# Splitting the value matmuls of a batch's last gate/value chunk into two column halves, each multiplied by its gate at once

## The chip, the cores and the metric

The kernel runs on one core of a Trainium2 chip. The metric is the time of one execution on the device in microseconds (us). Most executions of one kernel agree within about 0.3%, so medians of several runs are quoted. Kernels are compared only within the same rounds. A ratio is the mean time of one kernel's fast runs over that of the kernel before in the same rounds; it is therefore not quite the ratio of the medians quoted beside it.

The engines are named as in the profile: PE is TensorE's matmul, PEld its weight load, DVE is VectorE, ACT is ScalarE and POOL is GpSimd.

## The reference

Attention over eight batches (8 heads, 576 tokens, 16 beacon keys in front of the causal part), then a gated feed-forward block on the 4608 resulting rows:

```python
def _moe_ref(x, w_gate, w_val, w_out) -> np.ndarray:
    g = x @ w_gate
    inv_sqrt2 = np.float32(1.0 / np.sqrt(2.0))
    gelu = 0.5 * g * (1.0 + erf(g * inv_sqrt2))
    val = x @ w_val
    return (gelu * val @ w_out).astype(np.float32)
```

`x` is 4608 x 512, the gate and value weights are 512 x 1536. The kernel cuts the 1536 inner columns into 12 chunks of 128 (`fi` = 0 to 11) and the rows into groups of 512 (`CH`). There are nine such groups for eight batches.

## The kernel before

For one chunk of one group, four matmuls (`K_CHUNKS`) make the gate and four the value, each 128 x 512 in PSUM. ACT takes the GELU of the gate, and DVE multiplies value and gate into `hT_sb`, which the output matmuls (`o_ps`) read later.

```python
psum_s = ctx.enter_context(tc.tile_pool(name="psum_s", bufs=3, space=bass.MemoryType.PSUM))   # [P, 2, 512] f32 each: two banks
psum_t = ... bufs=1                                                            # one bank
psum_o = ... bufs=1                                                            # one bank
...
def part(ci, fi, w, ps, kks=range(K_CHUNKS), last=True):
    n0 = ci * CH
    for kk in kks:
        mm(ps, (wg_sb, wv_sb)[w][:, kk, fi * P : (fi + 1) * P],
           xT_sb[:, kk, n0 : n0 + CH], kk == 0, last and kk == kks[-1], ...)
...
def gated(ci, fi, v_ps, ge_sb):
    ...
    keep(nc.vector.tensor_tensor(out=h_of[ci][:, fi, :], in0=v_ps, in1=ge_sb, op=ALU.mult))
...
def gates_first(ci, *fis):
    ge_of = {}
    for fi, (pool, tag) in zip(fis, ((psum_t, "t"), (psum_o, "o"))):
        g_ps = pool.tile([P, CH], FP32, name="g_ps", tag=tag)
        part(ci, fi, 0, g_ps)
        ge_of[fi] = gelu(g_ps)
    for fi in fis:
        v_ps = psum_s.tile([P, 2, CH], FP32, name="v_ps", tag="s")[:, 0, :]
        part(ci, fi, 1, v_ps)
        gated(ci, fi, v_ps, ge_of[fi])
```

`gates_first` runs for chunks 10 and 11 of batches 1 to 6, so in six places. Right after it, PE goes on to the output matmuls of the same group and the attention scores (`s_ps`) of the next batch. The first three score groups take the three `psum_s` buffers in rotation; the third takes the one that chunk 11's value leaves.

The softmax here doesn't subtract the row's maximum and nothing guards it: scores larger than these inputs give would overflow.

## Time and profile before

| | before |
|---|---|
| median | 365.4 us (364.5 to 365.8, 3 runs at first) |
| profiled span | 363.6 us |
| PE busy | 353.7 us, 97% of the span |
| DVE, ACT, POOL busy | 45%, 53%, 44% |
| period from one place to the next | 38.78 to 38.95 us |

A busy share is an average over stages and does not say what sets the pace in one of them. A matmul's start is recorded and its end is modelled, so stalls of PE are measured below from start to start: when the next matmul would have started at the steady rate, and when it did.

### The profile page before, as it was taken

To read this page: it belongs to the slowest core of one execution; us is meant where nothing else is said; L and a number is where in the kernel's file an instruction comes from. 1 tells how busy PE (TensorE), PEld (TensorE's weight loads), DVE (VectorE), ACT (ScalarE), POOL (GpSimd) and SP (SyncE) were. 2 spreads that over 40 slices of the span, in tenths; PEclk is the share of its full clock that TensorE was granted. 3 is DMA by queue.
4 is the path that set the end of the run, shared out by engine and by line. 5 is a ranking of instruction groups with operands and counts; after the bars stand their busy time and mean duration, and the time that the engine had idled before them with its cause. 6 is when DMAs were issued, how large, how long until landed. Compare 5 with 4: busy or idle time off the path is not lost.

```text
span 363.6 us, 7732 instructions
## 1 busy us (share of the span) xinstructions
PE 353.7 (97%) x3164; PEld 187.5 (52%) x3206; DVE 163.4 (45%) x320; ACT 193.0 (53%) x252; POOL 161.3 (44%) x288
## 2 busy tenths in 40 slices
PE   7899999999999999999999999999999999999996
PEld 7664546444654455445644564446544554444443
DVE  3548746344453345434534354335443453333322
ACT  3975788237923694358633891379335953321210
POOL 8934387556536552945374545565330530000000
PEclk9999999999999999999999999999999999999999
DMA  8999999899289975999299927993795142000112
GB/s 112 174 203 204 196 121 97 125 156 199 30 128 135 215 58 71 168 217 62 56 138 205 138 38 122 162 198 35 111 147 127 15 65 113 0 2 29 58 38 108
DMA packets 160419, 41.57 MB, mean 114 GB/s; under 512 B 146944, under 2 KB 155904, under 8 KB 160384
## 3 DMA queue, kind: packets, MB, share of 16 engines
q0 software_dynamic: 104848, 19.11, 68.4%
q1 hardware_dynamic: 55536, 21.96, 30.9%
q8 instruction: 25, 0.41, 0.5%
q14 instruction: 10, 0.08, 0.1%
HBM read 38.27 MB, written 9.44 MB: 131 GB/s over the span
## 4 chain that ended last, share of the span: by engine, by line
PE 88%; DMA 5%; DVE 3%; POOL 2%; issue 1%; ACT 0%; SPq 0%; POOLq 0%
PE gv_ps L168 40%; PE o_ps L168 25%; PE x_ps L168 9%; PE s_ps L168 6%; DMA q_sb<-in_q_dram 3%; PE v_ps L168 3%; PE g_ps L168 3%; PE t_ps L176 2%; DMA k_sb<-in_k_dram 1%; DVE qkT L235 1%; POOL v_sb L111 1%; PE w_ps L168 1%; DVE o_sb L481 1%; DMA xT_sb<-y_sb 1%; POOL k_sb L111 0%
## 5 line engine op out<-in xcount | busy, mean ns | idle before, releaser
L171 ACT ACTIVATE ge_sb<-gv_ps 128x512 bf16<-128x512 f32 x95 | 55.8, 597 | 134.7 <-PE gv_ps L168 132.4
L433 DVE TENSOR_TENSOR hT_sb<-gv_ps,ge_sb 128x512 bf16<-128x512 f32 x95 | 64.9, 691 | 105.4 <-ACT ge_sb L171 105.3
L171 ACT ACTIVATE expT<-s_ps 128x992 bf16<-128x992 f32 (+3 forms) x112 | 100.5, 975 | 11.3 <-PE s_ps L168 9.8
L168 PE MATMUL gv_ps<-xT_sb,wg_sb 128*128 128x512 bf16 x378 | 105.1, 379 | 0.5
L168 PE MATMUL o_ps<-wo_sb,hT_sb 128*128 128x512 bf16 (+3 forms) x492 | 101.0, 373 | 2.3 <-DVE o_sb L481 0.9
L168 PE MATMUL gv_ps<-xT_sb,wv_sb 128*128 128x512 bf16 x364 | 101.7, 379 | 0.4
L320 POOL TENSOR_SCALAR_AFFINE_SELECT expT<-expT 128x256 bf16<-128x256 bf16 (+1 forms) x140 | 52.4, 391 | 48.4 <-ACT expT L171 47.1
L168 PEld LDWEIGHTS <-wv_sb 128*128 128x128 bf16 x432 | 42.2, 98 | 50.6
L168 PEld LDWEIGHTS <-wg_sb 128*128 128x128 bf16 x432 | 42.1, 98 | 49.9
L168 PEld LDWEIGHTS <-hT_sb 128*128 128x128 bf16 (+1 forms) x516 | 40.8, 96 | 43.8 <-issue 5.4
L168 PEld LDWEIGHTS <-expT 128*128 128x128 bf16 (+1 forms) x960 | 33.7, 97 | 9.0 <-POOL expT L320 3.1
L168 PE MATMUL x_ps<-v_sb,expT 128*128 128x65 bf16 (+1 forms) x960 | 36.8, 193 | 0.0
L111 POOL DMA_DIRECT2D v_sb<-in_v_dram x40 | 33.7, 861 | 6.1 <-DMA wv_sb<-in_moe_w_val_dram 2.4
L168 PE MATMUL s_ps<-qkT 64*128 64x80 bf16 (+5 forms) x528 | 33.1, 250 | 2.4 <-DVE qkT L239 1.6
L111 POOL DMA_DIRECT2D k_sb<-in_k_dram x30 | 25.2, 843 | 16.8 <-DMA v_sb<-in_v_dram 8.3
L111 POOL DMA_DIRECT2D q_sb<-in_q_dram x30 | 25.3, 874 | 9.9 <-DMA wo_sb<-in_moe_w_out_dram 3.6
L356 DVE TENSOR_TENSOR y_sb<-x_ps,r_sb 128x320 bf16<-128x320 f32 (+1 forms) x47 | 28.8, 612 | 1.8 <-DVE r_sb L354 0.2
L354 DVE RECIPROCAL r_sb<-x_ps 128x5 f32<-128x5 f32 (+1 forms) x47 | 9.6, 204 | 38.9 <-PE x_ps L168 38.9
L479 DVE COPY o_sb<-o_ps 128x512 f32<-128x512 f32 (+2 forms) x31 | 20.7, 668 | 13.3 <-PE o_ps L168 12.7
L168 PEld LDWEIGHTS <-qkT 64*128 64x128 bf16 x528 | 18.6, 95 | 14.0 <-issue 6.1
L399 POOL COPY hold_sb<-xT_sb 128x2 bf16<-128x2 bf16 x6 | 1.1, 186 | 31.9 <-DMA xT_sb<-y_sb 31.9
L433 DVE TENSOR_TENSOR hT_sb<-v_ps,ge_sb 128x512 bf16<-128x512 f32 x13 | 9.0, 692 | 9.5 <-PE v_ps L168 9.5
(58 smaller groups left out, 153.7 us busy)
## 6 DMA issues: line engine op xcount, KB each, us to landing
out_dram<-o_sb SPq DMA_DIRECT2D x35, 256.0 KB, 7.0
v_sb<-in_v_dram POOLq DMA_DIRECT2D x24, 128.0 KB, 9.2
q_sb<-in_q_dram POOLq DMA_DIRECT2D x18, 128.0 KB, 12.8
k_sb<-in_k_dram POOLq DMA_DIRECT2D x18, 128.0 KB, 5.5
wo_sb<-in_moe_w_out_dram POOLq DMA_DIRECT2D x3, 512.0 KB, 14.6
wg_sb<-in_moe_w_gate_dram POOLq DMA_DIRECT2D x2, 512.0 KB, 11.3
wv_sb<-in_moe_w_val_dram POOLq DMA_DIRECT2D x2, 512.0 KB, 13.1
v_sb<-in_v_dram POOLq DMA_DIRECT2D x8, 112.0 KB, 5.7
```

The lines of the kernel that those rows point to most:

```text
L111: keep(nc.gpsimd.dma_start(out=out_ap, in_=in_ap))
L168: keep(nc.tensor.matmul(out_ap, lhsT, rhs, start=start, stop=stop, **kw))
L171: keep(nc.scalar.activation(out_ap, in_ap, func, **kw))
L176: keep(nc.tensor.transpose(out_ap, in_ap, ident[0:n, 0:n]))
L235: keep(nc.vector.tensor_copy(out_ap, in_ap))
L320: nc.gpsimd.affine_select(out=d, in_=d, pattern=[[0, 2], [1, n]], compare_op=ALU.is_ge, fill=0.0, base=0, channel_multiplier=-1,)
L354: keep(nc.vector.reciprocal(r, x[:, :, :, D:DV]))
L356: nc.vector.tensor_tensor(out=y_of[i][:, :, h0:h1, :].rearrange("p j b d -> p b j d"), in0=x[:, :, :, 0:D], in1=r.to_broadcast([P, h1 - h0 ...
L399: keep(nc.gpsimd.tensor_copy(hold_sb, x[:, 0 : S : S - 1]))
L433: keep(nc.vector.tensor_tensor(out=h_of[ci][:, fi, :], in0=v_ps, in1=ge_sb, op=ALU.mult))
L479: keep(nc.vector.tensor_copy(o_ap, o_ps))
L481: keep(nc.vector.tensor_copy(o_ap, o_half))
```

## The change

Its intent: DVE should begin on chunk 11 as soon as half of it is there, so that the last product ends earlier and its PSUM buffer comes free earlier for the next batch's scores.

```diff
-    def part(ci, fi, w, ps, kks=range(K_CHUNKS), last=True):
+    def part(ci, fi, w, ps, kks=range(K_CHUNKS), last=True, c0=0, c1=CH):
...
-                xT_sb[:, kk, n0 : n0 + CH],
+                xT_sb[:, kk, n0 + c0 : n0 + c1],
...
-        keep(nc.vector.tensor_tensor(out=h_of[ci][:, fi, :], in0=v_ps, in1=ge_sb, op=ALU.mult))
+        keep(nc.vector.tensor_tensor(out=h_of[ci][:, fi, c0:c1], in0=v_ps, in1=ge_sb, op=ALU.mult))
...
-            part(ci, fi, 1, v_ps)
-            gated(ci, fi, v_ps, ge_of[fi])
+            for c0, c1 in ((0, CH),) if fi == fis[0] else ((0, CH // 2), (CH // 2, CH)):
+                part(ci, fi, 1, v_ps[:, c0:c1], c0=c0, c1=c1)
+                gated(ci, fi, v_ps[:, c0:c1], ge_of[fi][:, c0:c1], c0, c1)
```

More of the change, by code (lines that the diff above doesn't have):

```diff
@@ L428, in gelu, with gated @@
         return ge_sb
-    def gated(ci, fi, v_ps, ge_sb):
+    def gated(ci, fi, v_ps, ge_sb, c0=0, c1=CH):
         if ci not in h_of:
             h_of[ci] = hpool.tile([P, F_TILES, CH], BF16, name="hT_sb", tag="hT_sb")
-        keep(nc.vector.tensor_tensor(out=h_of[ci][:, fi, :], in0=v_ps, in1=ge_sb, op=ALU.mult))
+        keep(nc.vector.tensor_tensor(out=h_of[ci][:, fi, c0:c1], in0=v_ps, in1=ge_sb, op=ALU.mult))
     def gv_mms(ci, fi, *kks, last=False):
```

## The prediction

> **What bounds the kernel now.** I read the page first, then the chain of work by line, then the same chain in order of time, then five equal stretches of it, and last the timeline around one place that the change edits.
>
> ```profile
> PE 353.7 (97%) x3164; PEld 187.5 (52%) x3206; DVE 163.4 (45%) x320; ACT 193.0 (53%) x252; POOL 161.3 (44%) x288
> ...
> PE 88%; DMA 5%; DVE 3%; POOL 2%; issue 1%; ACT 0%; SPq 0%; POOLq 0%
> ```
>
> TensorE (PE) is busy for 97% of the span and makes up 88% of the chain that ended last. A busy PE is not yet a saturated one, so I also looked at whether anything else sets the pace from batch to batch. The next lines are the windows view, cut where the first gate matmul (g_ps) of the edited chunk pair starts in batches 1 to 6; columns are the stretch, its length, then each engine's busy time.
>
> ```profile
> 82.57:121.36 38.79, 38.36 (x345) 20.17 (x348) 17.13 (x33) 22.23 (x28) 22.25 (x39) 1.00 1.24 131
> 121.36:160.14 38.78, 38.35 (x344) 20.12 (x348) 17.14 (x33) 22.23 (x28) 21.34 (x38) 1.00 1.21 134
> 160.14:198.92 38.78, 38.35 (x344) 20.16 (x348) 17.14 (x33) 22.23 (x28) 20.89 (x38) 1.00 1.18 114
> 198.92:237.70 38.78, 38.35 (x344) 20.11 (x348) 17.13 (x33) 22.23 (x28) 20.79 (x38) 1.00 1.23 128
> 237.70:276.65 38.95, 38.52 (x344) 19.98 (x348) 17.29 (x33) 22.18 (x28) 15.85 (x32) 1.00 1.23 132
> ```
>
> Four periods agree to 0.01 us while POOL's work, which issues the loads, differs by over 1 us between them. A steady period with changing load work says that the loop through PE, ACT and DVE sets the time and no load does. That matters because the chain as printed runs through loads of q and k from 142 to 168 us; I take that part as an artefact of following POOL's queue back, since PE has no gap there.
>
> Now the edited place. The chain in order of time, for batch 2 (start, length, work):
>
> ```profile
> 121.36 1.73 PE g_ps L168 x8
> 123.09 1.73 PE v_ps L168 x8
> 124.81 0.54 PE o_ps L168 x4
> 125.35 0.71 PE s_ps L168 x14
> ```
>
> Both gate groups, both value groups (chunks 10 and 11), then the output matmuls of the same batch and the scores of the next follow without a gap: 8 matmuls in 1.73 us is 216 ns each. The timeline of the same place:
>
> ```profile
> 122.92 1.89 PE L168 MATMUL v_ps<-xT_sb,wv_sb 128*128 128x512 bf16 x8
> ...
> 124.06 0.69 DVE L433 TENSOR_TENSOR hT_sb<-v_ps,ge_sb 128x512 bf16<-128x512 f32 x1 [1.34 <-PE v_ps L168]
> 124.75 0.61 PE L168 MATMUL o_ps<-wo_sb,hT_sb 64*128 64x512 bf16 x4
> 124.92 0.69 DVE L433 TENSOR_TENSOR hT_sb<-v_ps,ge_sb 128x512 bf16<-128x512 f32 x1 [0.17 <-PE v_ps L168]
> ...
> 125.67 5.44 ACT L171 ACTIVATE expT<-s_ps 128x1024 bf16<-128x1024 f32 x6 [0.65 <-PE s_ps L168]
> ```
>
> The reader is to see three things. The two products on DVE start 0.1 us after their last matmul ends and nearly touch (124.75 against 124.92). PE does not wait for either: the output matmuls start at 124.75, before the second product has even begun. And ACT waits 0.65 us for PE's scores, so whatever delays PE here delays the softmax too.
>
> **What the Trainium skill says.** "PSUM — Partial Sum Buffer", section "PSUM bank collisions raise a hardware error", says that two engines must not touch one bank on the same 32 partitions at once, disjoint columns included, and to guard by bank, not by address. The value tile of chunk 11 is 512 fp32 columns; the page's section "Specifications (TRN2)" gives a bank as exactly 512 fp32 values, so both halves lie in one bank. The trace of before cannot show this case, because there no bank is read while more matmuls for it are to come. "VectorE: DVE Perf Modes", section "The TRN2 errata", gives (N+151)/0.96 ns for a one-element-per-cycle two-input operation. The trace agrees: 692 ns for 512 columns of the product (formula 691), and for the other product out of PSUM, 492 ns at 320 and 824 ns at 640 columns (formula 491 and 824). "TensorE: Matmul & The Clock Gate", section "Back-to-back issue gap", gives N/2.4 + 2.5 ns for a matmul at full clock, 216 ns at 512, as the chain above shows, and so 109 ns at 256; the granted clock is 1.00 in all five windows.
>
> ```profile
> L356 DVE TENSOR_TENSOR y_sb<-x_ps,r_sb 128x320 bf16<-128x320 f32 x30 | 14.8, 492 | 1.2 <-DVE r_sb L354 0.2
> L356 DVE TENSOR_TENSOR y_sb<-x_ps,r_sb 128x640 bf16<-128x640 f32 x17 | 14.0, 824 | 0.6
> ```
>
> **The change part by part.** It acts where gates_first is called: batches 1 to 6, chunk 11 only, so six places.
>
> Removed: per place 4 value matmuls of 512 columns and one product of 512 columns. Added: 8 matmuls of 256 columns, 4 more weight loads, two products of 256 columns. On PE that is 8 x 109 = 872 ns against 4 x 216 = 864 ns, about +0.01 us. The weight loads lie under the matmuls: the kernel already runs 30 x_ps matmuls of 65 columns, each with its own 128-column load, in 1.02 us, 34 ns apiece. On DVE, 2 x 425 = 850 ns against 692.
>
> Moved: the first half's product is in front of the second half's matmuls in program order. The built program, listed with its waits, has a new wait at the first matmul of the second half; counting the increments of that semaphore, it is released by the first half's product. So the read and the next write of the one bank are in sequence:
>
> ```
> Matmult v_ps<-xT_sb,wv_sb 128x256 [waits DVE]
> ```
>
> Its cost, in batch 2's times. The chunk 11 matmuls start at 123.79 (122.92 + 4 x 0.216). Four of 256 columns are issued until 124.22; the last starts at 124.11 and ends about 0.28 us later, which is the mean of the 256-column score matmuls, at 124.39. DVE is then still busy with chunk 10's product until 124.75. The first half's product starts at about 124.79 (0.04 us from one DVE operation to the next, as between the reciprocal and y_sb) and ends 0.425 us later at 125.21. From the end of a DVE operation to the matmul that waited for it takes 0.06 us, from the one such wait that recurs in this trace (o_sb ends at 128.94, the matmul starts at 129.00):
>
> ```profile
> 128.25 0.69 DVE L481 COPY o_sb<-o_ps 128x512 f32<-128x512 f32 x1 [2.64 <-PE o_ps L168]
> ...
> 129.00 1.45 PE L168 MATMUL o_ps<-wo_sb,hT_sb 128*128 128x512 bf16 x5 [0.16 <-DVE o_sb L481]
> ```
>
> So the second half starts at 125.27 in place of 124.22: PE idles for 1.05 us. All of it is on the path: before, PE went straight on to the output matmuls. With 0.01 us for the extra matmuls a place costs 1.06 us.
>
> What could be won in return is an earlier end of the last product, for whoever waits for its PSUM buffer: the third score group of the next batch (three buffers in rotation). Before, the product ended at 125.61, and that score group could start at about 125.63. There is thus at most some 0.05 us to win. After, the second half's matmuls end at about 125.88, its product runs from about 125.98 to 126.40, and the shifted score group comes at about 126.7. It is not waited for, but it was hardly waited for before. I take the gain as 0 to 0.05 us, 0.02 in the sum.
>
> Sum: 6 x (1.05 + 0.01 - 0.02) = 6.2 us. 365.4 + 6.2 = **371.6 us**, 1.7% longer.
>
> **The rivals.** First, that the intent holds: two halves let DVE start 0.43 us sooner and the next batch's scores get their buffer sooner. Against it: DVE is not free to start sooner (chunk 10's product holds it until 124.75), and nobody on PE waits for chunk 11's product. Even with no wait between the halves the gain would be at most 6 x 0.05 = 0.3 us: 365.1 us. Second, that the stall is partly hidden: behind PE's later waits for ACT, or behind loads. For it: ACT runs six exponentials without a gap after this place. Against it: ACT itself starts from PE's scores, idle 0.65 us before, so it shifts along; and the periods do not depend on the loads. If half were hidden the time would be 368.5 us. Third, that the stall is larger than worked out: a slower restart of PE after draining, or a slower hand-over between engines for this pair. 0.2 us more in each place gives 372.8 us, just beyond 2%. What speaks against it is the 0.06 us hand-over, seen with the same two engines.
>
> **Range and chances.** The wait is certain (it stands in the built program) and its length comes from durations that repeat to a few ns, so the spread is that of hidden parts and of the runs (1.3 us between lowest and highest). A range from 369.6 (a third hidden) to 373.0 (0.23 us more per place) should hold it 8 times in 10. The 2% line lies at 372.7. Faster by over 2%: 0.01. Within 2%: 0.86. Slower by over 2%: 0.13.
>
> **What would show it right or wrong.** Right: in the waits of PE a new row, v_ps waiting for DVE hT_sb, six times and about 1.0 us each, some 6 us in all; products of 256 columns at about 425 ns, 12 of them; the period between places 39.8 us; ACT idle before the first exponentials about 1.7 us in place of 0.65. Wrong: if the row is there but the period is still 38.8, the stall was hidden (second rival). If the row is missing, or far below 6 us, the wait was met early and my reading of DVE's order is wrong. If the period is over 40.0 with the row near 6 us, there is a cost after the stall that I did not see.

## The result

The changed kernel takes 370.28 us (median of 4 runs, 369.9 to 370.5) against 365.51 us, a ratio of 1.0134 with a 95% interval of 1.0117 to 1.0150. It is slower by 4.8 us, which is 0.80 us in each of the six places, and by the 2% measure it counts as the same. The time lies in the predicted range, 1.3 us below the predicted value.

The waits of PE, in the changed kernel, have a new row at the top (columns: who waited for whom, us in total, times, the longest):

```profile
PE v_ps L168 <- DVE hT_sb L433: 4.7, 6, 1.0
```

Six waits, all of the value matmuls for a product. The timeline of the same place in batch 2 of the changed kernel:

```profile
123.20 1.46 PE L168 MATMUL v_ps<-xT_sb,wv_sb 128*128 128x512 bf16 x8
...
124.33 1.02 DVE L433 TENSOR_TENSOR hT_sb<-v_ps,ge_sb 128x512 bf16<-128x512 f32 x2 [1.34 <-PE v_ps L168]
125.41 0.60 PE L168 MATMUL v_ps<-xT_sb,wv_sb 128*128 128x256 bf16 x4 [0.75 <-DVE hT_sb L433]
...
125.94 0.61 PE L168 MATMUL o_ps<-wo_sb,hT_sb 64*128 64x512 bf16 x4
126.05 0.43 DVE L433 TENSOR_TENSOR hT_sb<-v_ps,ge_sb 128x256 bf16<-128x256 f32 x1 [0.69 <-PE v_ps L168]
126.38 0.80 PE L168 MATMUL s_ps<-qkT 64*128 64x512 bf16 x14
...
126.86 1.02 ACT L171 ACTIVATE expT<-s_ps 128x1024 bf16<-128x1024 f32 x1 [1.56 <-PE s_ps L168]
```

The reader is to see that the eight value matmuls of before have become a run of eight (chunk 10 and the first half of chunk 11), a hole, and a run of four. The hole ends 0.06 us after the first half's product (124.33 + 1.02 = 125.35, then 125.41). ACT's idle time before the first exponential has grown from 0.65 to 1.56 us, so the softmax has shifted along with PE. From start to start, the first half begins at 124.06 (123.20 + 4 x 0.216) and is issued by 124.50 (4 x 0.109 later); the second half starts at 125.41. That is a stall of 0.91 us. The profile's own figure for this wait, 0.75, counts only from the modelled end of the last matmul.

The chain in order of time of the changed kernel shows which product ended it:

```profile
123.36 0.88 PE v_ps L168 x4
...
124.33 0.39 DVE hT_sb L433
124.73 0.22 issue
124.94 0.43 DVE hT_sb L433
125.37 0.04 issue
125.41 0.60 PE v_ps L168 x4
126.01 0.54 PE o_ps L168 x4
126.55 0.63 PE s_ps L168 x14
```

DVE has entered a chain that was PE alone before. Chunk 10's product runs to 125.02, and the first half's product stands behind it, from 124.94. The last line is the one gain: the block of 14 score matmuls takes 0.63 us, against 0.71 in the same view of before. In the timelines, from the block's start to the next output matmul, it is 0.63 (126.38 to 127.01) against 0.69 us (125.19 to 125.88).

The periods, in the windows view of the changed kernel cut at the same matmul as before:

```profile
82.01:121.64 39.63, 38.80 (x353) 20.29 (x352) 17.21 (x34) 22.24 (x28) 23.10 (x40) 1.00 1.22 132
121.64:161.27 39.63, 38.80 (x353) 20.28 (x352) 17.21 (x34) 22.24 (x28) 21.38 (x38) 1.00 1.21 122
161.27:201.11 39.84, 38.79 (x353) 20.28 (x352) 17.30 (x34) 22.24 (x28) 20.98 (x38) 1.00 1.18 118
```

The first two periods are 0.84 and 0.85 us longer than before, the fourth and fifth, not printed, too (39.63 and 39.79 us), and the granted clock is still 1.00. This agrees with the parts: 0.91 (stall) + 0.01 (eight smaller matmuls) - 0.06 (score block) = 0.86. The third is longer by another 0.21 us. There the two products on DVE took 1.24 us together in place of 1.02, because the second began 0.21 us later. In that stretch POOL issued three loads of k for 2.48 us without a break, but this alone does not delay DVE: at the first place of the run with two tiles (below), POOL issued four loads for 3.49 us without a break across the products, and they took their usual 1.35 us; at its third place they took 1.56. The run with two banks has the same 0.21 us at its third place and nowhere else. The cause stays open.

Six times 0.84 and the 0.21 are 5.3 us. The two profiled spans differ by 4.5, because in this run of the changed kernel the first place happened to come 0.56 us earlier (82.01 against 82.57), and the stretch from the last place to the end grew by 0.62 us only. The stretch before the first place holds no changed instruction; over all profiled runs it took from 82.0 to 83.6 us.

### The profile page after: what moved, and what is told of

Read it like the earlier page. It is cut to its first block, busy times and chain, and to the rows that moved or that the text cites. A ratio compares the mean times of both kernels' runs of the same rounds, so it can differ in the third digit from the quotient of the medians.

```text
span 368.1 us, 7822 instructions
## 1 busy us (share of the span) xinstructions
PE 355.7 (97%) x3230; PEld 187.7 (51%) x3230; DVE 163.6 (44%) x326; ACT 193.2 (52%) x252; POOL 161.5 (44%) x288
## 4 chain that ended last, share of the span: by engine, by line
PE 82%; DMA 8%; POOL 5%; DVE 3%; issue 2%; DVEq 0%; POOLq 0%
PE gv_ps L168 39%; PE o_ps L168 25%; PE x_ps L168 7%; PE s_ps L168 5%; DMA wo_sb<-in_moe_w_out_dram 4%; DMA qk<-in_q_dram 4%; PE g_ps L168 3%; PE v_ps L168 2%; POOL qk L111 1%; DVE hT_sb L433 1%; DVE o_sb L482 1%; POOL v_sb L111 1%; POOL q_sb L111 1%; POOL wg_sb L111 1%; POOL wv_sb L111 1%
## 5 line engine op out<-in xcount | busy, mean ns | idle before, releaser
L168 PE MATMUL gv_ps<-xT_sb,wv_sb 128*128 128x512 bf16 x380 | 105.3, 379 | 0.0
L168 PE MATMUL o_ps<-wo_sb,hT_sb 128*128 128x512 bf16 (+3 forms) x516 | 104.7, 373 | 0.5
L168 PEld LDWEIGHTS <-wv_sb 128*128 128x128 bf16 x456 | 44.6, 98 | 55.3 <-issue 5.7
L168 PEld LDWEIGHTS <-hT_sb 128*128 128x128 bf16 (+1 forms) x516 | 39.9, 96 | 43.1 <-issue 4.3
L168 PEld LDWEIGHTS <-qkT 64*128 64x128 bf16 x528 | 17.8, 95 | 14.3 <-issue 5.9
L168 PE MATMUL v_ps<-xT_sb,wv_sb 128*128 128x256 bf16 (+1 forms) x76 | 13.4, 311 | 4.7 <-DVE hT_sb L433 4.7
L433 DVE TENSOR_TENSOR hT_sb<-v_ps,ge_sb 128x256 bf16<-128x256 f32 (+1 forms) x19 | 9.5, 521 | 12.7 <-PE v_ps L168 12.6
```

What stands on the lines that cost most here:

```text
L168: keep(nc.tensor.matmul(out_ap, lhsT, rhs, start=start, stop=stop, **kw))
L433: keep(nc.vector.tensor_tensor(out=h_of[ci][:, fi, c0:c1], in0=v_ps, in1=ge_sb, op=ALU.mult))
```

## The experiments

My theory was that the cost is the stall alone: PE waits until DVE has done chunk 10's product and the first half's. The rivals were that the smaller matmuls and products cost the time, and that the stall is only the first half's own way through DVE, without the queue. All eleven runs gave correct results. "Period" is the distance from the first place to the second in the profile, or the mean over two where the chain view leaves one out; before it is 38.79 us.

| run | median us | before, same rounds | ratio (95% interval) | period us |
|---|---|---|---|---|
| two banks, one tile | 370.05 | 365.33 | 1.0130 (1.0111 to 1.0149) | 39.63 |
| two tiles | 364.40 | 365.33 | 0.9975 (0.9960 to 0.9991) | 38.73 |
| matmuls split only | 365.35 | 365.33 | 0.9997 (0.9982 to 1.0013) | 38.79 |
| chunk 10 in between | 365.00 | 365.33 | 0.9987 (0.9968 to 1.0006) | 38.73 |
| products split only, in four | 366.16 | 365.09 | 1.0030 (1.0012 to 1.0048) | 38.99 |
| 128 columns first | 370.80 | 365.09 | 1.0155 (1.0135 to 1.0175) | 39.71 |
| 384 columns first | 370.12 | 365.09 | 1.0136 (1.0116 to 1.0157) | 39.60 |
| both chunks split | 374.17 | 365.09 | 1.0243 (1.0219 to 1.0267) | 40.23 |
| two tiles, again | 364.92 | 365.14 | 0.9990 (0.9977 to 1.0002) | 38.72 |
| chunk 10 in between, again | 364.80 | 365.14 | 0.9987 (0.9974 to 1.0001) | 38.73 |
| chunk 10 split alone | 369.54 | 365.14 | 1.0120 (1.0106 to 1.0133) | 39.54 |

### The halves in two banks of one tile

```diff
-            v_ps = psum_s.tile([P, 2, CH], FP32, name="v_ps", tag="s")[:, 0, :]
-            for c0, c1 in ...:
-                part(ci, fi, 1, v_ps[:, c0:c1], c0=c0, c1=c1)
+            v_ps = psum_s.tile([P, 2, CH], FP32, name="v_ps", tag="s")
+            for g, (c0, c1) in enumerate(...):
+                part(ci, fi, 1, v_ps[:, g, 0 : c1 - c0], c0=c0, c1=c1)
...
```

> The changed kernel, but the two halves of chunk 11 lie in two different PSUM banks of the same tile. Theory A (the wait guards the bank): the stall goes, PE's waits for hT_sb vanish, and the time is about 365.2 us (the kernel before, less up to 0.06 us in each of six places). Theory B (the wait is the framework's, kept for a whole tile whatever its banks; the built program still has it, released by the first half's product): six waits of 0.75 to 0.9 us remain and the time equals the changed kernel, 370.3 us within 0.7. Theory C (the cost is not the wait but the smaller matmuls and products): also 370.3 us, but then the run with two tiles costs the same.

370.05 us, as changed. The stall is the same to the hundredth: the second half starts 2.21 us after chunk 10's first matmul in both kernels (123.83 to 126.04 here). Its timeline:

```profile
126.04 0.60 PE L168 MATMUL v_ps<-xT_sb,wv_sb 128*128 128x256 bf16 x4 [0.75 <-DVE hT_sb L433]
```

The two halves lie in different banks and the wait stays. So in this program the tile is enough to bring the wait: the write of the second half waits for the read of the first, though it lies in another bank. A rule for the one bank is not needed to explain the wait.

### The halves in two tiles

```diff
         for fi in fis:
-            v_ps = psum_s.tile([P, 2, CH], FP32, name="v_ps", tag="s")[:, 0, :]
             for c0, c1 in ((0, CH),) if fi == fis[0] else ((0, CH // 2), (CH // 2, CH)):
-                part(ci, fi, 1, v_ps[:, c0:c1], c0=c0, c1=c1)
+                v_ps = psum_s.tile([P, 2, CH], FP32, name="v_ps", tag="s")[:, 0, 0 : c1 - c0]
+                part(ci, fi, 1, v_ps, c0=c0, c1=c1)
...
```

> The same four plus four matmuls and two products, but each half of chunk 11 in a PSUM tile of its own (the second one takes the buffer that chunk 9 left). The built program then has no wait between the halves. Stall theory: no PE wait for the first half's product, period back to 38.7 to 38.8 us, time 365.2 us (before less at most 6 x 0.06 us plus 6 x 0.01 us). Rival (smaller matmuls and products cost the time): 370 us as changed.

364.40 us. The same matmuls and products as in the changed kernel, and the whole loss is gone; this settles that the loss was the wait. In the timeline all twelve value matmuls run through, the three products stand one behind the other, and the scores follow on time:

```profile
122.32 1.90 PE L168 MATMUL v_ps<-xT_sb,wv_sb 128*128 128x512 bf16 x12
123.45 1.35 DVE L433 TENSOR_TENSOR hT_sb<-v_ps,ge_sb 128x512 bf16<-128x512 f32 x3 [1.34 <-PE v_ps L168]
124.15 0.61 PE L168 MATMUL o_ps<-wo_sb,hT_sb 64*128 64x512 bf16 x4
124.60 0.79 PE L168 MATMUL s_ps<-qkT 64*128 64x512 bf16 x14
```

The score block is again 0.63 us long (124.60 to 125.23) and the period is 0.06 us shorter than before. Six times that is 0.36 us, but the runs were 0.93 us faster. Of the 1.1 us by which the profiled span is shorter, 0.54 lie before the first place (82.03 against 82.57 us). The repetition below deals with the difference.

### The matmuls split, one product

```diff
             for c0, c1 in ((0, CH),) if fi == fis[0] else ((0, CH // 2), (CH // 2, CH)):
                 part(ci, fi, 1, v_ps[:, c0:c1], c0=c0, c1=c1)
-                gated(ci, fi, v_ps[:, c0:c1], ge_of[fi][:, c0:c1], c0, c1)
+            gated(ci, fi, v_ps, ge_of[fi])
```

> Only the matmuls of chunk 11 are split, then one product of 512 columns over both halves. Stall theory: no wait between the halves, eight matmuls of 256 columns take 0.01 us more than four of 512, so 365.6 us, same as before within 0.3 us. Rival (the extra weight loads and restarts cost PE time): up to 370 us.

365.35 against 365.33 us, and the period is that of before. In the timeline the scores start 2.28 us after the first value matmul (122.41 to 124.69), against 2.27 before, so eight matmuls of 256 columns with eight weight loads cost 0.01 us more than four of 512 with four, as predicted.

### Chunk 10 between the two halves

```diff
-        for fi in fis:
-            v_ps = ...
-            for c0, c1 in ...:
-                part(...); gated(...)
+        v_of = {fi: psum_s.tile([P, 2, CH], FP32, name="v_ps", tag="s")[:, 0, :] for fi in fis}
+        f0, f1 = fis
+        for fi, c0, c1 in ((f1, 0, CH // 2), (f0, 0, CH), (f1, CH // 2, CH)):
+            part(ci, fi, 1, v_of[fi][:, c0:c1], c0=c0, c1=c1)
+            gated(ci, fi, v_of[fi][:, c0:c1], ge_of[fi][:, c0:c1], c0, c1)
```

> First half of chunk 11, then the whole of chunk 10, then the second half of chunk 11. The wait between the halves stays in the program, but 0.86 us of other matmuls lie in between: the first half's product would be over about 1.13 us after the first half began and the second half comes 1.30 us after it. Stall theory: the wait is met, none is seen, time 365.2 us (and the third score group finds its buffer free, 0.06 us gained in each place). If the wait has a cost of its own even when met, or the split costs, 366 us or more.

365.00 us, ratio 0.9987. The wait between the halves is still in the program, but the first half's product ends at 123.59 (123.17 + 0.42) and the second half is due at 123.64 (122.34 + 1.30), so it is met just in time. No wait for `hT_sb` is left in the waits of PE. A wait that was met cost nothing that shows here. It was met more narrowly than expected: the product was over 1.25 us after the first half began, not 1.13, because it waited for ACT's GELU of chunk 11, and not for PE:

```profile
123.17 0.42 DVE L433 TENSOR_TENSOR hT_sb<-v_ps,ge_sb 128x256 bf16<-128x256 f32 x1 [1.03 <-ACT ge_sb L171]
```

### The products split, the matmuls whole

```diff
-            for c0, c1 in ((0, CH),) if fi == fis[0] else ((0, CH // 2), (CH // 2, CH)):
-                part(ci, fi, 1, v_ps[:, c0:c1], c0=c0, c1=c1)
-                gated(ci, fi, v_ps[:, c0:c1], ge_of[fi][:, c0:c1], c0, c1)
+            part(ci, fi, 1, v_ps)
+            step = CH if fi == fis[0] else CH // 4
+            for c0 in range(0, CH, step):
+                gated(ci, fi, v_ps[:, c0 : c0 + step], ge_of[fi][:, c0 : c0 + step], c0, c0 + step)
```

> Matmuls of chunk 11 unsplit, its product in four quarters of 128 columns after them, so that the last one ends about 0.2 us later. Theory that the third score group already waits some 0.06 us for this product's buffer in the kernel before: PE loses the same 0.2 us in each of six places, 366.6 us, seen as a longer block of 14 score matmuls (0.9 us in place of 0.69 from its start to the next output matmul). Rival (nobody waits for chunk 11's product): 365.5 us as before.

366.16 against 365.09 us: 1.07 us slower, with 1.1 expected. Its timeline:

```profile
124.64 0.89 DVE L433 TENSOR_TENSOR hT_sb<-v_ps,ge_sb 128x128 bf16<-128x128 f32 x4 [0.17 <-PE v_ps L168]
124.91 1.07 PE L168 MATMUL s_ps<-qkT 64*128 64x512 bf16 x14
...
125.58 0.26 PEld L168 LDWEIGHTS <-qkT 64*128 64x128 bf16 x8 [0.36 <-DVE hT_sb L433]
```

The four quarters take 0.89 us, 0.20 more than one product, and end at 125.53; the weight loads of the last eight score matmuls, the third group, wait for that until 125.58. The score block takes 0.90 us (124.91 to 125.81), 0.21 more than before. So the third score group waits for chunk 11's product already in the kernel before, by about 0.06 us (0.69 us for the block, against 0.63 where nothing holds it), and the delay of that product by 0.20 us was paid in full. What the change set out to gain is there, and is no more than that.

### The split at 128 and at 384 columns

```diff
-            for c0, c1 in ((0, CH),) if fi == fis[0] else ((0, CH // 2), (CH // 2, CH)):
+            for c0, c1 in ((0, CH),) if fi == fis[0] else ((0, CH // 4), (CH // 4, CH)):          # one run
+            for c0, c1 in ((0, CH),) if fi == fis[0] else ((0, 3 * CH // 4), (3 * CH // 4, CH)):  # the other
```

> Split at 128 columns: 128 first, then 384. Queue theory (the first part's product stands behind chunk 10's product on DVE, then itself, then 0.06 us to PE): restart 2.08 us after chunk 10's first matmul, the first part is issued at 1.09: stall 0.99 us in each place, longer than in the changed kernel although the product is shorter; about 370.9 us. Rival (the stall is only drain plus product plus hand-over of the first part itself): about 0.62 us in each place, 369.0 us.

> Split at 384 columns: 384 first, then 128. Queue theory: the first part is issued 1.51 us after chunk 10's first matmul, its product (558 ns, from 1.78) ends at 2.34, restart 2.40: stall 0.89 us in each place, less than with 128 first by 0.1 us; about 370.3 us. Rival without the queue: more than with 128 first by about 0.27 us.

370.80 and 370.12 us. With 128 columns first, the first part is issued by 124.71 (123.62 + 0.864 + 4 x 0.056) and the second starts at 125.70, a stall of 0.99 us. With 384 first it is issued by 124.90 (123.39 + 0.864 + 4 x 0.1625) and the second starts at 125.79, a stall of 0.89 us. The restart in each of the two timelines:

```profile
125.70 0.81 PE L168 MATMUL v_ps<-xT_sb,wv_sb 128*128 128x384 bf16 x4 [0.83 <-DVE hT_sb L433]
125.79 0.38 PE L168 MATMUL v_ps<-xT_sb,wv_sb 128*128 128x128 bf16 x4 [0.72 <-DVE hT_sb L433]
```

Both stalls are as the queue theory had them. The shorter product has the longer stall, because it stands behind chunk 10's product while PE has less left to do. The rival had them the other way round.

### Chunk 10 split alone, and both chunks split

```diff
-            for c0, c1 in ((0, CH),) if fi == fis[0] else ((0, CH // 2), (CH // 2, CH)):
+            for c0, c1 in ((0, CH),) if fi != fis[0] else ((0, CH // 2), (CH // 2, CH)):   # chunk 10 alone
+            for c0, c1 in ((0, CH // 2), (CH // 2, CH)):                                   # both
```

> Only chunk 10 is split, so its first half finds DVE free, as in the first of the two stalls of the run with both chunks split. Stall start to start 1.19 - 0.44 = 0.75 us, no gain at the third score group because chunk 11's product is whole: 6 x (0.75 + 0.01) = 4.6 us, 369.8 us. Rival (a split costs the same wherever it is, 0.91 us): 370.9 us.

> Both chunks 10 and 11 split in halves, twice the dose. Chunk 10's first half finds DVE free: drain 0.16 us, 0.10 us to DVE, product 0.425, hand-over 0.06, so a stall of 0.75 us. Chunk 11's first half then finds DVE just free again: again 0.75. Sum 1.50 us per place, 12 waits of PE for hT_sb in all, time 374.2 us (365.5 + 6 x (1.50 + 0.02 - 0.06)). Rival (a fixed cost per place, not per split): 370.3 us. If each split cost the same as in the changed kernel: 375.1 us.

369.54 us (4.4 slower, 4.6 expected) and 374.17 us (expected 374.2). The waits of PE in the run with both:

```profile
PE v_ps L168 <- DVE hT_sb L433: 7.4, 12, 0.9
```

Twelve waits in place of six. In its timeline the second half of chunk 10 starts at 125.61 where 124.86 was due, and that of chunk 11 at 127.23 where 126.48 was due. Each stall is 0.75 us: 0.27 until DVE starts (124.86 to 125.13), a product of 0.42 and the hand-over of 0.06. The run with chunk 10 alone has the same stall once per place; its second half starts at 124.68 where 123.93 was due:

```profile
124.68 1.46 PE L168 MATMUL v_ps<-xT_sb,wv_sb 128*128 128x256 bf16 x8 [0.58 <-DVE hT_sb L433]
```

Where DVE is free a half costs 0.75 us; the 0.91 us of the changed kernel has 0.16 us of queue behind chunk 10's product in it.

### The two faster kernels once more

> The kernel with the halves in two tiles once more, beside the one with the order changed, on one chip. The six places account for 6 x 0.06 = 0.36 us less than before. The first run of it showed 0.9 us less. If that was the spread of runs, this run is 0.1 to 0.6 us below before and level with the other order; if two tiles gain something outside the six places, it is again some 0.9 us below before and 0.5 us below the other order.

> The other order (chunk 11's first half, chunk 10, chunk 11's second half) once more: 0.36 us below before by its six places, as in its first run (0.33).

Two tiles came out at 364.92 us (ratio 0.9990), and chunk 10 in between at 364.80 us (0.9987), against 365.14 us. Both came out 0.1% below, which is what their six places account for. The 0.93 us of the first run of two tiles was not seen again, so the part of it beyond 0.36 us is put down to the spread of the runs. Only that first run's interval excludes 1.0. Both versions are clearly faster than the changed kernel. That they beat the kernel before shows in the periods (38.72 and 38.73 against 38.79 us); in the times of single runs it is hardly clear of the noise.

## Why the prediction was right, and which term was off

**PE sets the pace, the loads do not.** Right. The stall went into the period almost in full, ACT shifted along, and the clock stayed at 1.00. Only the third period showed an addition, of 0.21 us.

**The smaller matmuls cost nothing.** Right: the run with only the matmuls split has ratio 0.9997.

**A wait at the second half, on the path, six times.** Right, seen six times; the two-tiles run shows that it was the whole cost. The reason given for it is not needed: the prediction said one bank, and the two-banks run shows that this program keeps the order within one tile across two banks. Whether the chip would allow the two at once in one bank was not tried, since such a kernel has a race.

**The size of the stall.** Predicted 1.05 us, measured 0.91. The failing term is "starts at about 124.79 (0.04 us from one DVE operation to the next, as between the reciprocal and y_sb)". The reciprocal feeds y_sb; the two products do not depend on each other, and the second then starts 0.08 us before the first ends (124.94 against 125.02). With that the restart comes 2.21 us after chunk 10's first matmul, not 2.35. The timeline of before had shown it, in a stretch that I had read for other reasons, for two such products:

```profile
107.78 1.29 DVE L433 TENSOR_TENSOR hT_sb<-gv_ps,ge_sb 128x512 bf16<-128x512 f32 x2 [2.96 <-ACT ge_sb L171]
```

Two products of 0.69 us in 1.29 us overlap by 0.09. That dependence is what parts the two spacings is read from such pairs, not tested by a run of its own; the trace of before bears it out for these kinds of pair: all 46 y_sb products that follow their reciprocal, and the six o_sb sums that follow their copy, start 0.03 us after its end, while the nine pairs of gate/value products that run one behind the other all overlap. The other terms on the path held: 0.42 us for the product, and 0.06 us of hand-over.

**The gain at the third score group.** Put at 0.02 us from a possible 0.05, measured 0.06 in the changed kernel and again in both faster ones. Both errors have the same sign: 6 x (0.14 + 0.04) is 1.1 of the 1.3 us by which the prediction was too high. So nothing cancelled by luck between these two; what is left, and the 0.21 us of the third place, are within the spread of the runs.

**The rivals.** The intent alone, without the wait, was put at 0.3 us at most, a little low. The two kernels that realise it gain 0.36 us by their periods, and 0.4 to 0.5 us by the ratios of three of their four runs. Nothing of the stall was seen hidden, and it was shorter than worked out, not longer; even the longer one of the third period was 0.91 + 0.21 = 1.12 us.

**The signs to look for.** The new row was there six times, with 4.7 us in place of some 6; part of that is the view's way of counting (0.16 us less per wait), which the prediction overlooked. The twelve products of 256 columns took 421 ns on average, 425 predicted. The period was 39.63 (39.8 predicted), ACT's idle time 1.56 (1.7).

## What to carry to other kernels

Before splitting an operation so that its consumer can begin sooner, look in the built program for a wait that the consumer's read puts before the producer's next write; give each half its own tile, or put other work between the halves. Then ask whether the consumer is free at that moment and whether anyone waits for its end: here it was busy, and the most that could be won was 0.06 us a place. To size a queue on one engine, take the spacing from a pair of operations with the same dependency, not from a pair in which one feeds the other.

## What the Trainium skill lacked or had wrong

- "VectorE: DVE Perf Modes", section "The DRAIN you can't avoid": it says that a next operation which is not held starts earlier, but gives no size. Here independent products overlap in the profile by 0.08 to 0.09 us (0.69 and 0.42 us in 1.02, two of 0.69 in 1.29, and four of 128 columns, 284 ns each, in 0.89 us).
- "TensorE: Matmul & The Clock Gate", section "Back-to-back issue gap": it gives about 131 ns per matmul of 512 columns for a stream in which each has its own weight load, and says that N/2.4 + 2.5 over-counts there. In such a stream this kernel takes 216 ns each (8 in 1.73 us), as that formula says.
- "Perfetto Trace Analysis", section "DVE / Act Engine Instruction (TENSOR_ADD, Activation, etc)": it shows the hand-over of a semaphore as a stage outside the profiled window, with no figure. From the end of a DVE product to the start of the matmul that waited for it, these runs show 0.06 us (125.35 to 125.41).
- No page says that a program may keep the order between a read of a tile and a later write to another bank of it; the two-banks run shows it, with 370.05 us against 364.40 for two tiles.
